# Opening the bilinear layer in the experts' memory slots: the change, the profile before it, and what it should do to the time

## The chip, the core and the metric

The kernel is one program on one core of a Trainium2 chip. The core has a matrix engine (TensorE, here PE), a vector engine (VectorE, DVE), an activation engine (ScalarE, ACT), a general engine (GpSimd, POOL) and a queue engine that issues transfers (SyncE, SP); each runs its own instructions in order, and they wait for each other through semaphores. Operands lie in on-chip memory in tiles, which are taken from pools: a pool has a fixed number of slots for a tag, and a new tile of that tag waits until the last reader of the tile that had the slot is done. The metric is device time in microseconds (us) of one launch, median of several runs.

## The reference

Three layers follow each other: attention of 8 batches against 32 state rows, a mixture of 8 experts in which each of 4352 rows goes to one expert, and the bilinear layer, with which this document is mostly concerned.

```
def _moe_ref(x, w_gate, w_output_gate, w1, w2):      # x: 4352 x 512
    ...                                               # e_idx: the expert of each row, with two gates
        h = np.maximum(x[mask] @ w1[e], 0.0)          # 512 -> 1024
        ye = h @ w2[e]                                # 1024 -> 512
        out[mask] = gate_w[mask, None] * eom[mask, e, None] * ye
def _moe2_ref(x, w1, w2, w3, w_out):
    a = x @ w1                                        # 512 -> 1024
    b = x @ w2
    h = a * b @ w3                                    # 1024 -> 1024
    return (h @ w_out).astype(np.float32)             # 1024 -> 512
```

Everything is float32, but for the weights of the bilinear layer, which are passed as float64.

## The kernel before, in words

**Arithmetic.** A float32 product is made of three PE passes over halves: `split` (L177, L178) makes a rounded half on ACT (a CAST) and the remainder on DVE, and `passes` (L183) multiplies high by high, high by low and low by high. The two last matrices of the bilinear layer are multiplied together beforehand (`wo`, 1024 x 512), beside the attention.

**Experts.** Rows are sorted by expert and worked through in 10 units. A unit has a first matrix (`ph`, L183 into relu at L1013 and L1014) and a second (`py`). The results are copied by ACT to a tile `y` (L1064 in the last unit, L1076 in the others) and written to the array `y_T` by transfers that ACT issues. Expert weights are loaded raw by SP into `wr_raw` (tag `raw`, 3 slots) and split into pairs of half tiles of 128x2x512 elements, which lie in two rings of slots, `wr0` (8 pairs) and `wr1` (4 pairs). Rows are gathered into tiles `xg` (4 slots).

**Bilinear operands.** `operands()` works in the gaps of the experts: in 16 steps it loads a piece of w1 and w2 as raw 64-bit words, converts it (L218 and L232 on ACT, more on DVE and POOL; tiles `wab`), forms the sums that the seven-product scheme of Strassen and Winograd wants, splits them (`wh_w`, `wh_s`) and writes them to `w_rows`, one row for each of the 8 values of f.

**Bilinear layer.** The 34 tiles of 128 rows are worked through in 5 blocks of 7, 7, 7, 7 and 6. `load_y` (L1254) loads a block of `y_T` in two tiles; `sums_of` (L1362) forms four differences t1 to t4 (on DVE in block 0, on POOL later) and splits seven operands x0 to x6. For each f (8 per block), `load_w` (L1332) brings the 1.79 MB of `w_rows` for that f (2 slots, each taken by the load two steps ahead), and `products` makes 7 products p1 to p7 of 6 PE passes each (42 matmuls of 448 columns), combines them (u2, u3, u4, a1, b1 on DVE; b2 L1412, a2 L1415 and the product `ab` L1416 on POOL; s1 and s5 are copied by ACT, L1403 and L1406) and splits `ab` in two parts: `aa` for 4 of the row tiles and `ab` for the others. `out_of` multiplies these by `wo` (`po`, 512 columns): 4 tiles x 3 passes = 12 per f follow one step of f behind, the other row tiles come at the end of the block. `written` scales a row tile to `o` (L1439 on ACT, L1441 on DVE; in a slot of `xg`) and scatters it to the output with a transfer that POOL issues (L1442).

**Memory and order.** The pools of the experts (`c3`, `c4`) are closed before the bilinear layer, whose nine pools `bl0` to `bl8` lie where they were. So a bilinear tile waits for those readers of expert tiles whose memory it has. The order of instructions on each engine is set when the program is built, by a scheduler that estimates when each is ready.

Of the kernel before, what the change touches and what calls it, by code (L numbers as in the profile page):

```python
# [9 lines left out]
F32 = mybir.dt.float32  # L10
# [42 lines left out]
def tile_attention_moe_bilinear(  # L53
# [137 lines left out]
    def load_f32(pool, name, src, tag, bufs, temps=None, tmp=2):  # L191

        src = src if isinstance(src, list) else [src]
# [12 lines left out]
        if not wide:  # L206
            return w
        words = raw.bitcast(I32).rearrange("p (n t) -> p n t", t=2)
# [94 lines left out]
    with ExitStack() as c1:  # L303
# [388 lines left out]
        c3 = ctx.enter_context(ExitStack())  # L692
        rings.append(Lines(c3.enter_context(tc.tile_pool(name="wr0", bufs=RING0, reuse_waits="tile"))))
# [176 lines left out]
    rings.append(Lines(c3.enter_context(tc.tile_pool(name="wr1", bufs=RING - RING0, reuse_waits="tile"))))  # L870
# [14 lines left out]
    with ExitStack() as c2:  # L885
# [56 lines left out]
        def operands():  # L942

            for f in range(KF):
                for kk in range(2):
                    wa_, wb_ = [
                        w.rearrange("(h m p) f -> m p h f", h=2, p=P)[kk][:, :, f * P : (f + 1) * P]
                        for w in (wa, wb)
                    ]
                    name = f"{f}_{kk}"  # L950
                    w = load_f32(
                        e3, "wab" + name, [wa_, wb_[:, 1], wb_[:, 0]], "wab", 1, None, 1
                    ).rearrange("p (m n) -> p m n", n=P)
                    a11, a12, a22, a21 = [w[:, i] for i in range(4)]
                    yield
                    sums = e3.tile([P, 4, P], F32, tag="top", name="sums" + name, bufs=1)
                    s1, s2, s3, s4 = [sums[:, i] for i in range(4)]
                    add = nc.gpsimd.tensor_tensor
                    add(s1, a21, a22, op=ALU.add)
                    add(s3, a11, a21, op=ALU.subtract)  # L960
                    add(s2, s1, a11, op=ALU.subtract)
                    add(s4, a12, s2, op=ALU.subtract)
                    halves(w[:, 0:3], (f, kk, 0), "w" + name)
                    yield
                    write_wab()
                    yield
                    halves(sums, (f, kk, 3), "s" + name)
                    yield
                    write_wab()
# [276 lines left out]

        def load_y(s):
# [64 lines left out]
    c3.close()  # L1312


    def bilinear(y, group):
# [5 lines left out]
        with ExitStack() as c5:  # L1321
            wp, ap, xp0, op0, xp1, op1, aap, abp, tp = [
                Lines(c5.enter_context(tc.tile_pool(name=f"bl{i}{group}", bufs=1, reuse_waits="tile")))
                for i in range(9)
            ]
            NB = max(BLOCKS) * P
            NH = NB // 2
            w_t, wo, raw_wo = {}, {}, {}

            def load_w(s, f):  # L1330
                t = wp.tile([P, 2, 2, NP, P], F32R, tag="w", name=f"w{s}_{f}", bufs=2)
                nc.sync.dma_start(out=t.bitcast(F32), in_=w_rows[f])  # L1332
                w_t[s, f] = t

            def load_wo(f):
                raw_wo[f] = wr_raw.tile([P, DM], F32, tag="raw", name=f"rwo{f}", bufs=RAW)
                nc.sync.dma_start(out=raw_wo[f], in_=wo_rows[f * P : (f + 1) * P])

            def split_wo(f):
                wo[f] = [  # L1340
                    p.tile([P, DM], F32R, tag="wo", name=f"wo{j}_{f}", bufs=KF)
                    for j, p in enumerate((op0, op1))
                ]
                split(*wo[f], raw_wo.pop(f))

            def sums_of(y, s):

                n = BLOCKS[s] * P // 2
                b11, b21, b12, b22 = [h[:, i : i + 2] for h in y for i in (0, 2)]
                x = {}  # L1350

                def put(i, src):
                    hl = [
                        (xp0 if i < 2 else xp1).tile([P, 2, NH], F32R, tag=f"x{i}_{j}", name=f"x{i}_{j}_{s}")
                        for j in range(2)
                    ]
                    x[i] = both(hl, slice(None), slice(None), slice(0, n))
                    split(*x[i], src)

                def less(i, a, b):  # L1360
                    t = wr_raw.tile([P, 2, NH], F32, tag="raw", name=f"t{i}_{s}", bufs=RAW)[:, :, 0:n]
                    (nc.vector if s == 0 else nc.gpsimd).tensor_tensor(t, a, b, op=ALU.subtract)  # L1362
                    return t

                t1 = less(1, b12, b11)
                t2 = less(2, b22, t1)
                put(0, b11)
                put(1, t1)
                t3 = less(3, b22, b12)
                put(2, t2)  # L1370
                t4 = less(4, t2, b21)
                put(3, t3)
                put(4, b21)
                put(5, b22)
                put(6, t4)
                return x

            A11, A12, A22, S1, S2, S3, S4 = range(NP)
# [165 lines left out]
```

## Time and profile before

| | us |
|---|---|
| runs | 1183.18, 1186.32, 1191.93 (median 1186.32) |
| profiled execution | 1187.32 |
| its span | 1185.4 |
| PE busy in the span | 1123.0 |
| granted clock of PE over the span | 0.982 of full speed |

The span is the time from the first to the last instruction that the profiler saw; the profiled execution took 1.9 us more than that. In the profile's views every instruction has the line of the source and the tiles it writes and reads (`p<-x,w`), a count of instructions (`x42`) and, in brackets, the idle time of the engine before it with what ended that. Rows of one kind that follow each other are put together. The experts lie from before 215 us to 634 us, the bilinear layer from 634 us to the end.

### The profile page before, as it was taken

How to read it: one execution, taken by the hardware profiler on the slowest of the kernel's cores; microseconds unless marked ns; L12 is line 12 of the kernel's file. 1: busy time of each engine (PE TensorE's matmuls, PEld its weight loads, DVE VectorE, ACT ScalarE, POOL GpSimd, SP SyncE). 2: the span in 40 equal slices, each digit the busy share in tenths (PEclk: the TensorE clock that was granted, in tenths of full speed). 3: DMA queues.
4: the chain of work that ended last, by engine and by line, in shares of the span. 5: the costliest groups of instructions: out<-in, count | busy, mean ns of one | idle time of the engine just before them, and what ended most of it. 6: DMA issues, size and time to landing. Idle time of an engine off the chain costs nothing. (4 is left out here: it accounts for less than half of the span.)

```text
span 1185.4 us, 18194 instructions
## 1 busy us (share of the span) xinstructions
PE 1123.0 (95%) x6880; PEld 986.2 (83%) x6880; DVE 660.9 (56%) x1206; ACT 448.7 (38%) x807; POOL 396.3 (33%) x383
## 2 busy tenths in 40 slices
PE   5888999999989999999997999999999999999994
PEld 4665777999989999878885888888888889889993
DVE  4999797535554647464752746343634544463441
ACT  3788544435454545454213223211321222132110
POOL 2655335113220412141000534532463363334331
PEclk9999999999999999999997999999999999999997
DMA  7776427547575666676114654544544445444431
GB/s 223 235 246 215 142 90 242 179 152 233 180 239 192 218 201 222 225 243 202 54 63 178 240 186 141 207 161 175 186 186 145 168 177 187 137 174 143 175 118 56
DMA packets 83040, 211.55 MB, mean 178 GB/s; under 512 B 12928, under 2 KB 40576, under 8 KB 77824
## 3 DMA queue, kind: packets, MB, share of 16 engines
q1 hardware_dynamic: 60288, 167.53, 41.2%
q10 hardware_dynamic: 17024, 24.42, 5.6%
q0 software_dynamic: 5632, 18.35, 4.6%
q8 instruction: 56, 0.92, 0.3%
q14 instruction: 40, 0.33, 0.1%
HBM read 166.23 MB, written 44.04 MB: 177 GB/s over the span
## 5 line engine op out<-in xcount | busy, mean ns | idle before, releaser
L183 PE MATMUL p<-x,w 128*128 128x448 f32 (+1 forms) x1680 | 350.2, 363 | 8.7 <-DMA w<-w_rows 7.1
L183 PEld LDWEIGHTS p<-x,w 128*128 128x128 f32 x1680 | 315.2, 190 | 35.9 <-issue 7.5
L183 PE MATMUL py<-h,w 128*128 128x288 f32 (+1 forms) x1152 | 199.6, 331 | 6.1 <-ACT y L1076 6.0
L183 PE MATMUL ph<-x,w 128*128 128x288 f32 (+2 forms) x1248 | 195.3, 316 | 0.8 <-DVE h L1014 0.8
L183 PEld LDWEIGHTS py<-h,w 128*128 128x128 f32 x1152 | 175.5, 190 | 22.5 <-ACT y L1076 7.7
L183 PEld LDWEIGHTS ph<-x,w 128*128 128x128 f32 x1248 | 179.4, 188 | 12.5 <-DVE h L1014 1.2
L1412 POOL TENSOR_TENSOR b<-u,s 128x448 f32<-128x448 f32 (+1 forms) x40 | 47.7, 1191 | 279.5 <-DVE u L1411 279.5
L178 DVE TENSOR_TENSOR w<-raw,w 128x1024 fp32r<-128x1024 f32 x80 | 96.7, 1236 | 76.0 <-ACT w L177 75.4
L183 PE MATMUL po<-wo,aa 128*128 128x512 f32 x480 | 123.1, 393 | 0.9 <-ACT aa L177 0.9
L183 PEld LDWEIGHTS po<-wo,aa 128*128 128x128 f32 x480 | 89.7, 188 | 18.0 <-ACT aa L177 1.5
L177 ACT CAST w<-raw 128x1024 fp32r<-128x1024 f32 x80 | 81.6, 1050 | 50.6 <-DMA raw<-in_moe_w 45.7
L177 ACT CAST ab<-ab 128x384 fp32r<-128x384 f32 (+1 forms) x40 | 19.7, 492 | 210.1 <-POOL ab L1416 210.1
L233 POOL TENSOR_TENSOR wab<-wab,wab_top 128x512 int32<-128x512 int32 x16 | 20.6, 1287 | 187.2 <-DVE wab_top L226 177.5
L183 PE MATMUL po<-wo,ab 128*128 128x512 f32 x336 | 79.6, 390 | 0.0
L183 PEld LDWEIGHTS po<-wo,ab 128*128 128x128 f32 x336 | 62.9, 188 | 13.3 <-DVE o L1441 0.2
L986 POOL DMA_INDIRECT xg<-x_rows,gidx x38 | 44.0, 1158 | 81.0 <-PE pxg L992 75.3
L1415 POOL TENSOR_TENSOR a<-u,s 128x448 f32<-128x448 f32 (+1 forms) x40 | 48.4, 1209 | 58.8 <-DVE u L1414 58.7
L1014 DVE SCALAR_TENSOR_TENSOR h<-ph,h 128x288 fp32r<-128x288 f32 (+2 forms) x104 | 51.1, 501 | 20.2 <-ACT h L1013 19.6
L1414 DVE TENSOR_TENSOR u<-u,p 128x448 f32<-128x448 f32 (+1 forms) x40 | 24.3, 607 | 64.1 <-PE p L183 63.9
L1013 ACT ACTIVATE h<-ph 128x288 fp32r<-128x288 f32 (+2 forms) x104 | 44.4, 446 | 40.3 <-PE ph L183 28.1
L183 PE MATMUL pwo<-wu,w3T 128*128 128x512 f32 x192 | 50.5, 413 | 3.4 <-POOL w3T L178 2.9
L1416 POOL TENSOR_TENSOR ab<-a,b 128x448 f32<-128x448 f32 (+1 forms) x40 | 50.1, 1252 | 3.1
(289 smaller groups left out, 1411.9 us busy)
## 6 DMA issues: line engine op xcount, KB each, us to landing
w<-w_rows SPq DMA_DIRECT2D x40, 1792.0 KB, 7.1
raw<-in_moe_w SPq DMA_DIRECT2D x80, 512.0 KB, 4.3
x<-in_x SPq DMA_DIRECT2D x32, 256.0 KB, 5.6
w_raw<-in_moe_w SPq DMA_DIRECT2D x16, 512.0 KB, 4.1
x_rows<-xr SPq DMA_DIRECT2D x32, 256.0 KB, 2.8
w_rows<-wh_s ACTq DMA_DIRECT2D x32, 256.0 KB, 2.0
y<-y_T SPq DMA_DIRECT2D x8, 896.0 KB, 6.6
w_rows<-wh_w ACTq DMA_DIRECT2D x32, 192.0 KB, 3.3
```

The source lines that it names most:

```text
L177: nc.scalar.copy(hi, src)
L178: (engine or nc.vector).tensor_tensor(lo, src, hi.bitcast(F32), op=ALU.subtract)
L183: m = nc.tensor.matmul(o, l[a], r[b], start=start and i == 0, stop=stop and i == 2)
L233: nc.gpsimd.tensor_tensor(wi, wi, top, op=ALU.add)
L986: gathered = nc.gpsimd.indirect_dma_start(out=x[0:r], out_offset=None, in_=x_rows, in_offset=bass.IndirectOffsetOnAxis(ap=gidx[0:r, t - s0 ...
L1013: nc.scalar.activation(hl[0], src, AF.Relu)
L1014: nc.vector.scalar_tensor_tensor(out=hl[1], in0=src, scalar=0.0, in1=hl[0].bitcast(F32), op0=ALU.max, op1=ALU.subtract)
L1412: gpsimd(b2, u3, s5, op=ALU.add)
L1414: vector(u4, u2, p3, op=ALU.add)
L1415: gpsimd(a2, u4, s5, op=ALU.add)
L1416: gpsimd(ab[:, n : 2 * n], a2, b2, op=ALU.mult)
```

## The change

The rings `wr0` and `wr1` stay open to the end, and five of the nine bilinear pools are gone. The operands x0 to x6 and the differences take pairs of slots in ring `wr0` (9 allocations per block on 8 slots), `wo` takes ring `wr1`, the raw `wo` rows and the temporaries u3 and u4 take `xg` slots (shared with output rows `o`), and a1, b1, a2, b2 and `ab` take `wr_raw` slots. A new `begin()` runs ahead of the last expert unit's second matrix: it loads block 0 of y, the `w_rows` of f = 0 in four pieces (three into `wr_raw`, one into `xg`) and makes the first half of block 0's operands. The bilinear layer then starts with the loads of f = 1 and f = 2. In `operands()` the raw load stands one gap ahead of its conversion. The code for more rows than usual takes the same calls and is left out below.

```diff
@@ load_f32 is split; the raw load can now stand apart from the conversion @@
+        return convert(*load_raw(pool, name, src, tag, bufs), pool, name, temps)
+
+    def load_raw(pool, name, src, tag, bufs):
...
+        return w, raw
+
+    def convert(w, raw, pool, name, temps=None):
+        if raw is w:
             return w
+        n = w.shape[1]
...
-        c3 = ctx.enter_context(ExitStack())
-        rings.append(Lines(c3.enter_context(tc.tile_pool(name="wr0", bufs=RING0, reuse_waits="tile"))))
+        rings.append(Lines(ctx.enter_context(tc.tile_pool(name="wr0", bufs=RING0, reuse_waits="tile"))))
...
-    rings.append(Lines(c3.enter_context(tc.tile_pool(name="wr1", bufs=RING - RING0, reuse_waits="tile"))))
+    rings.append(Lines(ctx.enter_context(tc.tile_pool(name="wr1", bufs=RING - RING0, reuse_waits="tile"))))
...
@@ operands @@
+            def loaded(f, kk):
...
+                return load_raw(e3, f"wab{f}_{kk}", [wa_, wb_[:, 1], wb_[:, 0]], "wab", 1)
+
+            each = list(itertools.product(range(KF), range(2)))
+            raw = loaded(*each[0])
+            yield
+            for i, (f, kk) in enumerate(each):
+                name = f"{f}_{kk}"
+                w = convert(*raw, e3, "wab" + name).rearrange("p (m n) -> p m n", n=P)
+                a11, a12, a22, a21 = [w[:, i] for i in range(4)]
+                yield
...
+                halves(w[:, 0:3], (f, kk, 0), "w" + name)
+                yield
+                write_wab()
+                if i + 1 < len(each):
+                    raw = loaded(*each[i + 1])
+                yield
+                halves(sums, (f, kk, 3), "s" + name)
+                yield
+                write_wab()
...
+        def pair(i, name):
+            return [rings[i].tile([P, 2, 512], F32R, tag=f"w{j}", name=f"w{j}_{name}") for j in range(2)]
+
...
+        def sums_of(y, s, x):
+
+            n = BLOCKS[s] * P // 2
+            b11, b21, b12, b22 = [h[:, i : i + 2] for h in y for i in (0, 2)]
+            less = lambda o, a, b: (nc.vector if s == 0 else nc.gpsimd).tensor_tensor(o, a, b, op=ALU.subtract)
+
+            def put(i, src):
+                x[i] = both(pair(0, f"x{i}_{s}"), slice(None), slice(None), slice(0, n))
+                split(*x[i], src)
+
+            t1, t2 = [t[:, :, 0:n].bitcast(F32) for t in pair(0, f"t12_{s}")]
+            less(t1, b12, b11)
+            less(t2, b22, t1)
+            put(0, b11)
+            put(1, t1)
+            put(2, t2)
+            yield
+            t3, t4 = [t[:, :, 0:n].bitcast(F32) for t in pair(0, f"t34_{s}")]
+            less(t3, b22, b12)
+            less(t4, t2, b21)
+            put(3, t3)
+            put(5, b22)
+            put(4, b21)
+            put(6, t4)
+
+        def begin():
+
+            y = load_y(0)
+            w = {}
+            for first, n in ((S1, 2), (S3, 2), (A11, 2), (A22, 1)):
+                if n == 2:
+                    t = wr_raw.tile([P, 2, 2, 2, P], F32R, tag="raw", name=f"wf{first}", bufs=RAW)
+                else:
+                    t = xp.tile([P, 2, 2, 1, P], F32R, tag="xg", name=f"wf{first}", bufs=BX)
+                nc.sync.dma_start(out=t.bitcast(F32), in_=w_rows[0][:, :, :, first : first + n])
+                w.update({first + i: t[:, :, :, i] for i in range(n)})
+            x = {}
+            todo = sums_of(y, 0, x)
+            next(todo)
+            return w, x, todo
...
-                    y0 = load_y(0)
                     for _ in fills:
                         pass
+                    begun = begin()
                 second_of(n)
...
-    c3.close()
...
-            wp, ap, xp0, op0, xp1, op1, aap, abp, tp = [
+            wp, tp, aap, abp = [
...
             def load_wo(f):
-                raw_wo[f] = wr_raw.tile([P, DM], F32, tag="raw", name=f"rwo{f}", bufs=RAW)
+                raw_wo[f] = xp.tile([P, DM], F32, tag="xg", name=f"rwo{f}", bufs=BX)
...
             def split_wo(f):
...
+                if f % 2 == 0:
+                    hl = pair(1, f"wo{f}")
+                    wo.update({f + i: both(hl, slice(None), i) for i in range(2)})
                 split(*wo[f], raw_wo.pop(f))
...
+                def temp(pool, tag, name, bufs=1):
+                    return pool.tile([P, 512], F32, tag=tag, name=f"{name}_{s}_{f}", bufs=bufs)[:, 0:n]
+
+                def temps(name):
+                    t = wr_raw.tile([P, 2, 512], F32, tag="raw", name=f"{name}_{s}_{f}", bufs=RAW)
+                    return t[:, 0, 0:n], t[:, 1, 0:n]
...
+                u3 = temp(xp, "xg", "u3", BX)
                 vector(u3, u2, p7, op=ALU.add)
+                a2, b2 = temps("ab2")
...
+                u4 = temp(xp, "xg", "u4", BX)
...
+                ab = wr_raw.tile([P, 1024], F32, tag="raw", name=f"ab_{s}_{f}", bufs=RAW)
...
+                a1, b1 = temps("ab1")
...
-            load_w(0, 0)
-            x = sums_of(y, 0)
             load_w(0, 1)
-            for f in range(RAW):
+            load_w(0, 2)
+            for _ in todo:
+                pass
+            for f in range(2):
                 load_wo(f)
...
-                        if f + RAW < KF:
-                            load_wo(f + RAW)
+                        if f + 2 < KF:
+                            load_wo(f + 2)
...
-                    if f + 2 < KF or more:
+                    if (f + 2 < KF or more) and (s or f):
...
-                    x = sums_of(y, s + 1)
+                    x = {}
+                    for _ in sums_of(y, s + 1, x):
+                        pass
...
-    bilinear(y0, "out")
+    bilinear(*begun, "out")
```

In the order of instructions, SP's rows at the end of the experts' loads, before (`raw_7` is the last expert's last weight, `y` and `w` belong to block 0, `rwo` is a raw row block of `wo`):

```order
301 L875 DMA raw_7_7044<-in_moe_w 128x2x512
302 L1254 DMA y_1_7425<-y_T 128x4x448
303 L1254 DMA y_0_7423<-y_T 128x4x448
304 L1332 DMA w_0_7579<-w_rows 128x3584
305 L1332 DMA w_1_7617<-w_rows 128x3584
306 L1337 DMA rwo_7619<-wo_rows 128x512
307 L1337 DMA rwo_7621<-wo_rows 128x512
```

and with the change (`wf` are the four pieces for f = 0):

```order
301 L881 DMA raw_7_7036<-in_moe_w 128x2x512
302 L1310 DMA wf_7433<-w_rows 128x4x128
303 L1310 DMA wf_7427<-w_rows 128x4x256
304 L1310 DMA wf_7429<-w_rows 128x4x256
305 L1310 DMA wf_7431<-w_rows 128x4x256
306 L1394 DMA rwo_7610<-wo_rows 128x512
307 L1394 DMA rwo_7612<-wo_rows 128x512
308 L1273 DMA y_1_7425<-y_T 128x4x448
309 L1273 DMA y_0_7423<-y_T 128x4x448
310 L1389 DMA w_1_7586<-w_rows 128x3584
311 L1389 DMA w_2_7588<-w_rows 128x3584
```

The four pieces and two `rwo` loads now stand ahead of the y loads, and the first whole `w` loads are those of f = 1 and 2.

ACT's rows in one expert unit (338 to 361 us of the trace), before (`wab_1` is an operand step, `py_0_288` the second column half of the unit's first output group, `raw` and `w` are weights of the coming unit):

```order
413 L1076 COPY y_0_4514<-py_0_0_4515 128x288
414 L177 CAST w_2_3_4501<-raw_3_4499 128x1024
415 L177 CAST x_12_4425<-pxg_4447 128x4x128
416 L177 CAST x_12_4425<-pxg_4456 128x4x128
417 L218 ACTIVATE wab_1_top<-wab_1_raw 128x512
418 L232 ACTIVATE wab_1_4683<-wab_1_raw 128x512
419 L1076 COPY y_0_4514<-py_0_288_4541 128x288
420 L1078 REGISTER_ALU
421 L1078 DMA y_T<-y_0_4514 128x576
422 L1076 COPY y_1_4570<-py_1_0_4571 128x288
```

and with the change:

```order
410 L177 CAST wh_s_0_4682<-sums_0_4558 128x512
411 L1087 COPY y_0_4505<-py_0_0_4506 128x288
412 L945 DMA w_rows<-wh_s_0_4682 128x512
413 L177 CAST x_12_4416<-pxg_4438 128x4x128
414 L177 CAST w_2_3_4492<-raw_3_4490 128x1024
415 L177 CAST x_12_4416<-pxg_4447 128x4x128
416 L945 DMA w_rows<-wh_s_0_4683 128x512
417 L1087 COPY y_0_4505<-py_0_288_4532 128x288
418 L225 ACTIVATE wab_1_top<-wab_1_raw 128x512
419 L239 ACTIVATE wab_1_4623<-wab_1_raw 128x512
```

The second copy of `y_0` stood behind both `wab_1` instructions and now stands ahead of them; a cast `wh_s_0` of the operand step before now stands ahead of the first copy.

POOL's rows at the end of block 0, before (`b`, `a` and `ab` with `_0_7` or `_7` belong to f = 7, `t_1` to block 1, `t_2` to block 2):

```order
227 L1412 TENSOR_TENSOR b_0_7_8308<-u_0_7_8303,s_0_7_8326 128x448
228 L1362 TENSOR_TENSOR t_1_8417<-t_1_8401,y_0_7813 128x896
229 L1415 TENSOR_TENSOR a_0_7_8306<-u_0_7_8304,s_0_7_8326 128x448
230 L1416 TENSOR_TENSOR ab_7_8309<-a_0_7_8306,b_0_7_8308 128x448
231 L1362 TENSOR_TENSOR t_2_9275<-y_1_8721,y_0_8719 128x896
232 L1442 DMA out<-o_8482,L 4352x512
233 L1442 DMA out<-o_8488,L 4352x512
234 L1442 DMA out<-o_8494,L 4352x512
235 L1362 TENSOR_TENSOR t_2_9277<-y_1_8721,t_2_9275 128x896
236 L1362 TENSOR_TENSOR t_2_9287<-y_1_8721 128x896
237 L1442 DMA out<-o_8500,L 4352x512
238 L1442 DMA out<-o_8506,L 4352x512
```

and with the change (`ab_0_7` stands for b2 and then a2; `w_t_1` are t3 and t4 of block 1 in a ring pair):

```order
226 L1280 TENSOR_TENSOR w_t_1_8380<-y_1_7796 128x2x448
227 L1280 TENSOR_TENSOR w_t_1_8381<-w_t_1_8365,y_0_7794 128x2x448
228 L1434 TENSOR_TENSOR ab_0_7_8308<-u_0_7_8306,s_0_7_8288 128x448
229 L1438 TENSOR_TENSOR ab_0_7_8308<-u_0_7_8317,s_0_7_8288 128x448
230 L1440 TENSOR_TENSOR ab_7_8320<-ab_0_7_8308 128x448
231 L1280 TENSOR_TENSOR w_t_2_9224<-y_1_8682,y_0_8680 128x2x448
232 L1467 DMA out<-o_8447,L 4352x512
233 L1467 DMA out<-o_8453,L 4352x512
234 L1280 TENSOR_TENSOR w_t_2_9225<-y_1_8682,w_t_2_9224 128x2x448
235 L1467 DMA out<-o_8459,L 4352x512
236 L1467 DMA out<-o_8465,L 4352x512
237 L1467 DMA out<-o_8471,L 4352x512
```

Before, one difference stood behind b2 of f = 7; now two stand ahead of it, and among the scatters there are two differences of block 2 (t1, t2) where there were three.

## Rows read from the trace of the kernel before

**Rows 1.** The page, part 1: busy time (us), share of span, instructions.

```profile
PE 1123.0 (95%) x6880; PEld 986.2 (83%) x6880; DVE 660.9 (56%) x1206; ACT 448.7 (38%) x807; POOL 396.3 (33%) x383
```

**Rows 2.** Waits of PE over the whole span: total us, times, longest us.

```profile
PE p L183 <- DMA w<-w_rows: 7.1, 1, 7.1
PE py L183 <- ACT y L1076: 6.0, 7, 2.5
```

**Rows 3.** Windows: busy us per engine, granted clock, DMA share, GB/s.

```profile
640.00:660.00 20.00, 17.41 (x59) 14.92 (x60) 9.85 (x13) 6.50 (x9) 3.82 (x3) 0.66 0.81 291
```

**Rows 4.** PE timeline: start, us, instruction, count, idle before; experts into bilinear layer.

```profile
621.19 12.74 PE L183 MATMUL py<-h,w 128*128 128x512 f32 x55
641.03 4.82 PE L183 MATMUL p<-x,w 128*128 128x448 f32 x12 [7.11 <-DMA w<-w_rows]
647.31 14.40 PE L183 MATMUL p<-x,w 128*128 128x448 f32 x54 [1.46 <-ACT x L177]
662.58 2.33 PE L183 MATMUL po<-wo,aa 128*128 128x512 f32 x9 [0.88 <-ACT aa L177]
...
685.37 2.44 PE L183 MATMUL po<-wo,aa 128*128 128x512 f32 x10
```

**Rows 5.** PE timeline: two later f steps of block 0.

```profile
696.71 2.48 PE L183 MATMUL po<-wo,aa 128*128 128x512 f32 x10
...
703.14 5.11 PE L183 MATMUL p<-x,w 128*128 128x448 f32 x24
708.08 2.48 PE L183 MATMUL po<-wo,aa 128*128 128x512 f32 x10
```

**Rows 6.** SP timeline: issues of the first weight loads.

```profile
633.79 0.83 SPq L1332 DMA_DIRECT2D w<-w_rows  x2
```

**Rows 7.** ACT timeline in the same stretch: issue of the first y_T write.

```profile
632.55 0.34 ACTq L1065 DMA_DIRECT2D y_T<-y  x1
```

**Rows 8.** DMA issues, 625 to 660 us: count, KB each, median us to landing.

```profile
y_T<-y ACTq DMA_DIRECT2D x4, 256.0 KB, 2.3
```

**Rows 9.** PE timeline inside one expert unit, 338 to 361 us.

```profile
343.10 3.42 PE L183 MATMUL py<-h,w 128*128 128x288 f32 x24 [0.51 <-ACT y L1076]
...
349.54 11.34 PE L183 MATMUL py<-h,w 128*128 128x288 f32 x72 [2.49 <-ACT y L1076]
```

**Rows 10.** ACT timeline beside it.

```profile
347.98 0.66 ACT L218 ACTIVATE wab_top<-wab_raw 128x512 f32<-128x512 f32 x1 [2.42 <-DMA wab_raw<-in_moe_w]
...
349.09 0.39 ACT L1076 COPY y<-py 128x288 f32<-128x288 f32 x1
```

**Rows 11.** POOL timeline at the end of block 0.

```profile
731.82 1.84 POOL L1412 TENSOR_TENSOR b<-u,s 128x448 f32<-128x448 f32 x1 [5.55 <-DVE u L1411]
733.62 2.97 POOL L1362 TENSOR_TENSOR t<-t,y 128x896 f32<-128x896 f32 x1
736.56 2.01 POOL L1415 TENSOR_TENSOR a<-u,s 128x448 f32<-128x448 f32 x1
738.65 1.89 POOL L1416 TENSOR_TENSOR ab<-a,b 128x448 f32<-128x448 f32 x1
749.57 2.12 POOL L1362 TENSOR_TENSOR t<-y,y 128x896 f32<-128x896 f32 x1 [9.03 <-DMA y<-y_T]
```

**Rows 12.** DVE timeline there.

```profile
730.01 1.09 DVE L178 TENSOR_TENSOR x<-y,x 128x896 fp32r<-128x896 f32 x1
731.03 0.62 DVE L1411 TENSOR_TENSOR u<-u,p 128x448 f32<-128x448 f32 x1
...
735.76 1.78 DVE L178 TENSOR_TENSOR x<-y,x 128x896 fp32r<-128x896 f32 x1 [0.36 <-ACT x L177]
...
754.76 0.75 DVE L1441 TENSOR_SCALAR o<-po,L 128x512 f32<-128x512 f32 x1 [3.69 <-DMA out<-o,L]
```

**Rows 13.** ACT timeline there.

```profile
740.57 0.52 ACT L177 CAST ab<-ab 128x384 fp32r<-128x384 f32 x1 [2.35 <-POOL ab L1416]
```

**Rows 14.** PE timeline there.

```profile
737.25 4.94 PE L183 MATMUL po<-wo,ab 128*128 128x512 f32 x21
```

More of the change, by code (lines that the diff above doesn't have):

```diff
@@ L205, in load_f32 @@
             nc.sync.dma_start(out=o, in_=a)
-        if not wide:
+        return w, raw
+    def convert(w, raw, pool, name, temps=None):
+        if raw is w:
             return w
+        n = w.shape[1]
         words = raw.bitcast(I32).rearrange("p (n t) -> p n t", t=2)
@@ L942, in operands @@
         def operands():
[L944 to L969, printed above, removed]
@@ new lines, in loaded @@
+            def loaded(f, kk):
+                wa_, wb_ = [
+                    w.rearrange("(h m p) f -> m p h f", h=2, p=P)[kk][:, :, f * P : (f + 1) * P]
+                    for w in (wa, wb)
+                ]
+                return load_raw(e3, f"wab{f}_{kk}", [wa_, wb_[:, 1], wb_[:, 0]], "wab", 1)
[7 more added lines that the diff above has]
+                yield
+                sums = e3.tile([P, 4, P], F32, tag="top", name="sums" + name, bufs=1)
+                s1, s2, s3, s4 = [sums[:, i] for i in range(4)]
+                add = nc.gpsimd.tensor_tensor
+                add(s1, a21, a22, op=ALU.add)
+                add(s3, a11, a21, op=ALU.subtract)
+                add(s2, s1, a11, op=ALU.subtract)
+                add(s4, a12, s2, op=ALU.subtract)
+                halves(w[:, 0:3], (f, kk, 0), "w" + name)
[7 more added lines that the diff above has]
+                write_wab()
@@ L1245, in tile_attention_moe_bilinear @@
         fills = itertools.chain(operands(), places())
+        NB = max(BLOCKS) * P
+        NH = NB // 2
+        A11, A12, A22, S1, S2, S3, S4 = range(NP)
+        def pair(i, name):
+            return [rings[i].tile([P, 2, 512], F32R, tag=f"w{j}", name=f"w{j}_{name}") for j in range(2)]
         def load_y(s):
@@ L1311, in tile_attention_moe_bilinear, with bilinear @@
         c4.close()
-    c3.close()
-    def bilinear(y, group):
+    def bilinear(w0, x, todo, group):
         with ExitStack() as c5:
-            wp, ap, xp0, op0, xp1, op1, aap, abp, tp = [
+            wp, tp, aap, abp = [
                 Lines(c5.enter_context(tc.tile_pool(name=f"bl{i}{group}", bufs=1, reuse_waits="tile")))
-                for i in range(9)
+                for i in range(4)
             ]
-            NB = max(BLOCKS) * P
-            NH = NB // 2
-            w_t, wo, raw_wo = {}, {}, {}
+            w_t, wo, raw_wo = {(0, 0): w0}, {}, {}
             def load_w(s, f):
@@ L1332, in load_w @@
                 nc.sync.dma_start(out=t.bitcast(F32), in_=w_rows[f])
-                w_t[s, f] = t
+                w_t[s, f] = [t[:, :, :, c] for c in range(NP)]
             def load_wo(f):
-                raw_wo[f] = wr_raw.tile([P, DM], F32, tag="raw", name=f"rwo{f}", bufs=RAW)
+                raw_wo[f] = xp.tile([P, DM], F32, tag="xg", name=f"rwo{f}", bufs=BX)
                 nc.sync.dma_start(out=raw_wo[f], in_=wo_rows[f * P : (f + 1) * P])
             def split_wo(f):
[L1340 to L1343, printed above, removed]
+                if f % 2 == 0:
+                    hl = pair(1, f"wo{f}")
+                    wo.update({f + i: both(hl, slice(None), i) for i in range(2)})
                 split(*wo[f], raw_wo.pop(f))
[L1346 to L1378, printed above, removed]
             def products(s, f, x):
@@ L1383, in products @@
                 w = w_t.pop((s, f))
-                def temp(pool, name, tag=None):
-                    return pool.tile([P, 512], F32, tag=tag or name, name=f"{name}_{s}_{f}", bufs=1)[:, 0:n]
                 def product(i, tag, c, name):
@@ L1512, in tile_attention_moe_bilinear @@
                 run(range(T0 + FEW, MAXT))
-        bilinear(load_y(0), "again")
+        bilinear(*begin(), "again")
 _INS = [
```

12 lines of the change are left out of this document (3 added, 9 removed).

## The prediction

> **What bounds the kernel now.** I read the busy times first: PE is busy 1123.0 of 1185.4 us [rows 1], so at most 62.4 us of waiting can go, and whatever is gained elsewhere only counts where PE waits for it. The list of PE's waits comes next. Most of its entries belong to the attention, which the change leaves alone; the two that it touches are the longest of all, 7.1 us for the first `w` of the bilinear layer, and 6.0 us in 7 pieces for ACT's copies of expert results, the longest 2.5 us [rows 2]. The windows add what waits alone don't tell: around 634 us PE is not only idle, its granted clock is 0.66 on the mean of 640 to 660 us, between the levels of 1.2 and 2.4 GHz [rows 3]. From 663.5 us to the end of the layer PE has no idle time, so there the change can only cost.
>
> The sum is made against the profiled execution, 1187.3 us, which is 1.0 above the median of the runs shown (1186.3).
>
> **1. From the experts into the bilinear layer.** The last `py` ends at 621.19 + 12.74 = 633.93. SP issues the two first `w` loads at 633.79, since their slots lie on expert memory that `py` still reads [rows 6], and the first product starts at 641.03, 7.24 us after that issue [rows 4]. Then PE waits 7.11, 1.46 and 0.88 us and runs slowly in between: 12 matmuls in 4.82 us [rows 4].
>
> How much of this stretch is work? By 685.37, where the `po` of f = 2 begin, PE has done f = 0, 1, 2 and the first 24 products of f = 3, and the `po` of f = 0 and 1: 150 products and 24 `po`. A later step (42 products, 12 `po`) takes 708.08 - 696.71 = 11.37 us; 24 products start at 703.14 and the next `po` at 708.08, so 4.94 us for 24 or 0.206 each, and the 12 `po` are 11.37 - 42 x 0.206 = 2.72 [rows 5]. Three steps, 24 products more and one set of `po` less: 3 x 11.37 + 4.94 - 2.72 = 36.3 us. It took 685.37 - 633.93 = 51.4. **15.1 us** can be won at most: 9.45 idle, the other 5.7 the low clock.
>
> With the change, the four pieces for f = 0 are issued ahead of the y loads, all the splits of block 0's operands stand on ACT ahead of the last `y` copies, and PE goes from the last `py` matmul into p1. Is the next thing late? f = 1 needs a whole `w` at 633.93 + 42 x 0.206 = 642.6. Its load still waits for `py`, is issued at about 633.9 and can be had 7.2 us later, at 641.1: 1.5 us to spare. f = 2 needs its load 11.4 us after that, and in the trace the second of two loads issued together held nothing up. The copies s1 and s5 now stand on ACT among the four `y` copies, of which there are two buffers: the third waits for the first transfer, issued at 632.55 [rows 7] and landed 2.3 us later [rows 8], 634.9; s1 follows at about 636 and PE wants it at 633.93 + 24 x 0.206 = 638.9. Two `rwo` blocks and the rest of `wo` are off the path. I take 14.5 us of the 15.1, 0.6 for a late piece; bounds 0 and 15.1. A loss is excluded, because the old loads at the old time are the worst that can be left.
>
> **2. The experts.** PE waits 2.49 us at 347.05 for a copy of `y` [rows 9]; ACT stood before `wab_top`, which waited 2.42 us for its raw words, and made the copy only at 349.09 [rows 10]. With the change that copy stands ahead of both `wab` instructions, so this wait goes. The 72 matmuls behind it took 11.34 us where 24 take 3.42 [rows 9], so 11.34 - 10.26 = 1.1 us of low clock may go too. On the other side the cast `wh_s` of the step before now stands ahead of the first copy. A cast of 384 columns takes 0.52 us [rows 13], so one of 512 some 0.6 by estimate, and the wait of 0.51 at 343.10 may grow by that. The raw transfers stay in their order on SP. Between 0 and -3.6 I take **-2.5 us**, about the value of the named wait plus half of what the clock and the new cast leave.
>
> **3. The ends of the blocks (4 times).** t3 and t4 of the next block now stand ahead of b2 of f = 7 on POOL, where only t4 stood behind it. In the trace u3 was made at 731.03 [rows 12] and POOL went b2 1.84, t4 2.97, a2 2.01, `ab` 1.89 [rows 11], and ACT cast at 740.57 [rows 13]. t3's slot comes free with p7, just ahead of u3, at about 730.9. A difference takes 2.12 alone and 2.97 beside DVE [rows 11]. So the chain ends after 2 x 2.12 to 2 x 2.97, then 1.84 to 2.01, 2.01 and 1.89: at 740.9 to 742.8, and the cast of 0.52 at 741.4 to 743.3. In the order with the change PE has 21 `po` and 8 products before it wants that cast; the 21 begin at 737.25 and end at 742.1 [rows 14], so with 8 x 0.206 at 743.75. The slack is 0.4 to 2.3 us. I cost this at 0; without that cover it is up to 2.97 each time.
>
> Next, u3 and u4 take `xg` slots that rows `o` also take, and wait for scatters. DVE has already waited 3.69 us there for one, with PE busy [rows 12]. Behind it on DVE stands u2 and everything PE's product banks wait for. Since t1 and t2 only, not three differences, now stand between the scatters, the fourth is issued at least 2.12 us earlier than before, which covers it. I put 0.2 us on each end, **+0.8** in all, out of 0 to 4 x (2.97 + 3.69) = 26.6.
>
> By the Trainium skill (SBUF — State Buffer, "SBUF: two separate sides") VectorE instructions with two on-chip inputs and GpSimd ones hold a shared pair of ports as an exclusive lock, and the other blocks fully. The trace agrees that they disturb each other, 1.09 against 1.78 us for a DVE remainder [rows 12]; by a full block the chain here would be longer than I sum it, and that is the third rival.
>
> **Sum.** 1187.3 - 14.5 - 2.5 + 0.8 = 1171.1, say **1171 us**; own range 1167 to 1175.
>
> **Rivals.**
> - *Half of the first gain stays away.* The clock is low anyway, or f = 1 waits because its load shares the transfer engines with the `y_T` writes. For: slack of only 1.5 us; DMA share 0.81 in the window that follows [rows 3]. Against: those writes ran beside the first `w` before as well. 1171.1 + 7.2 = 1178.
> - *Operands for f = 0 are not early.* The change doesn't do what it says if a piece waits for a slot until the last `py`. Then 7.1 us and the low clock stay, and only the expert part is won: 1187.3 - 2.5 = 1185. Against: the order has the pieces ahead of the y loads, and those ahead of the first whole `w`.
> - *Full blocking between DVE and POOL at the ends.* Four late remainders (x3, x5, x4, x6) of 1.09 us alternate with the five POOL instructions, so the chain is 4.4 us longer; less 0.8 of slack, 3.6 four times: 1171.1 + 14.4 = 1185. For: 1.78 instead of 1.09, 2.97 instead of 2.12. Against: these durations, in a stretch just like it, are already in my sum.
> - *Slower: scatters hold the next block's u3.* Place: DVE's first u3 of blocks 1 to 4. If the `ab` of f = 7 comes 2.97 late and u3 then finds its slot under a scatter still on its way, 3.69 more, PE stops behind full banks and pays the low clock, 1.1 as after the 2.49 us wait: 7.8 us four times is 31: 1202. It decides once the slack of 0.4 us is used up and a scatter lands more than about 2 us later than before.
>
> **Chances.** Forecast 0.63, half gain 0.14, not early 0.06, blocking 0.08, scatters 0.09. A measurement of this kernel can tell about 1%, 11.9 us. Faster by more needs less than 1174.4: nearly all of the forecast and a little of the half gain, 0.64. Within 1%: 0.28. Slower by over 1%: 0.08, the scatters. The range takes in the forecast with both of its ends, the half gain and part of the two at 1185: low 1171.1 - 0.6 - 1.1 - 0.8 - 3 for the spread of the runs, about 1165; high 1184.
>
> **What would show it.** Right: no wait of PE for `w` or `x` near 634, a granted clock near 1.00 from 620 to 660, PE at the `po` of f = 2 some 36.3 us after the last `py`; no 2.5 us wait in the expert unit; no PE idle at the four block ends. Wrong: a wait `p <- w` at about 642, `p <- s` at 639, `po <- ab` at a block end, or DVE waiting for `out` ahead of a u3 with PE idle behind it.

## The result and the profile after

The changed kernel takes **1171.74 us** (median of 4 runs, 1168.13 to 1172.81) where the kernel before takes 1186.97 beside it (4 runs): ratio 0.9864, 95% interval 0.9821 to 0.9907. The forecast was 1171. The profiled execution took 1172.32, its span 1170.1, so 15.3 us are gone from the span.

On the page, PE's busy time fell by 3.9 us [rows 1]; the rest of the 15.3 is waiting that is gone.

```profile
PE 1119.1 (96%) x6880; PEld 983.0 (84%) x6880; DVE 664.0 (57%) x1206; ACT 449.7 (38%) x807; POOL 397.0 (34%) x383
```

The list of PE's waits has no entry for `w` or `x` any more, and `py` is down from 6.0 us to 2.2 [rows 2]. `ph` has grown from 0.8 us to 2.8, and `po` has two waits, 1.0 and 0.8, where it had one of 0.9 [rows 4].

```profile
PE ph L183 <- DVE h L1025: 2.8, 4, 0.9
...
PE py L183 <- ACT y L1087: 2.2, 4, 1.0
...
PE po L183 <- ACT aa L177: 1.0, 1, 1.0
PE po L183 <- DVE aa L178: 0.8, 1, 0.8
```

**From the experts into the bilinear layer.** The windows of this stretch show the clock at its upper level throughout (the last three values are the clock, the DMA share and GB/s), where 640 to 660 us had 0.66 [rows 3].

```profile
620.00:640.00 20.00, 20.00 (x95) 17.43 (x94) 10.71 (x17) 7.00 (x10) 2.98 (x3) 1.00 0.46 173
640.00:660.00 20.00, 18.18 (x84) 15.39 (x84) 12.71 (x16) 5.76 (x11) 8.50 (x6) 1.00 0.76 288
```

PE's timeline answers to [rows 4]: from the last `py` PE goes straight into the 42 products of f = 0 (`wf` are the four early pieces) and the next 24, and the `po` of f = 2 begin at 669.71, which is 38.59 us after the last `py` (631.12) instead of 51.44. Here and below, where the products follow the last `py` at once, its end is taken as their start; the end that the profile models for it is 0.16 us later, so a start with a wait and one without can be compared only to within that.

```profile
619.90 11.38 PE L183 MATMUL py<-h,w 128*128 128x512 f32 x49
631.12 8.68 PE L183 MATMUL p<-w_x,wf 128*128 128x448 f32 x42
639.63 5.02 PE L183 MATMUL p<-w_x,w 128*128 128x448 f32 x24
645.64 1.22 PE L183 MATMUL po<-w_wo,aa 128*128 128x512 f32 x3 [0.98 <-ACT aa L177]
...
659.24 0.73 PE L183 MATMUL po<-w_wo,aa 128*128 128x512 f32 x2 [0.84 <-DVE aa L178]
...
669.71 2.23 PE L183 MATMUL po<-w_wo,aa 128*128 128x512 f32 x9
```

Who was late for the two `po`? For the first, ACT's timeline tells: the cast of `ab` and the cast `aa` behind it stood 10.27 us for a write of `y_T`, although the last such write had been issued at 633.89.

```profile
633.89 0.34 ACTq L1076 DMA_DIRECT2D y_T<-y  x1
644.55 0.51 ACT L177 CAST ab<-ab 128x384 fp32r<-128x384 f32 x1 [10.27 <-DMA y_T<-y]
644.97 0.61 ACT L177 CAST aa<-ab 128x512 fp32r<-128x512 f32 x1
```

SP had issued two whole `w` at 631.35 [rows 6], 2.5 us ahead of that write; the first y_T write was issued at 629.90, as early against the last `py` as in [rows 7]. The list of transfers of 625 to 662 us has the four writes at a median of 6.3 us, against 2.3 before [rows 8]. Neither median stands for all four: asked write by write, the trace with the change gives a landing for two, 2.1 us for the first, issued ahead of the loads, and 10.6 for the last; the trace before gives one, 2.3 for the write issued at 633.60, ahead of the loads, and none for the two issued behind them.

```profile
631.35 0.82 SPq L1389 DMA_DIRECT2D w<-w_rows  x2
```
```profile
y_T<-y ACTq DMA_DIRECT2D x4, 256.0 KB, 6.3
```

The second `po` has another cause. ACT's cast `aa` for it ends at 655.1; DVE is late with the remainder, because two remainders ahead of it took 2.49 and 2.61 us beside POOL's first two differences of block 1. With POOL idle such remainders take 0.56 us (at 711.02) and 0.69 (at 651.23). The remainder of `aa` then ends at 659.18, and PE goes on at 659.24.

```profile
653.36 2.27 POOL L1280 TENSOR_TENSOR w_t<-y,y 128x896 f32<-128x896 f32 x1 [2.14 <-DMA y<-y_T]
653.56 2.49 DVE L178 TENSOR_TENSOR ab<-ab,ab 128x384 fp32r<-128x384 f32 x1
655.71 2.32 POOL L1280 TENSOR_TENSOR w_t<-y,w_t 128x896 f32<-128x896 f32 x1
655.98 2.61 DVE L178 TENSOR_TENSOR w_wo<-rwo,w_wo 128x512 fp32r<-128x512 f32 x1
```

**The experts.** The `py` of [rows 9] runs without its wait, and its 72 matmuls take 10.13 us instead of 11.34. The price is in the next unit, where PE waits for `h`, and ACT stands twice ahead of a relu (`h`): for the raw words, 2.58 us where it was 1.24 before (at 382.64, with no wait of PE), and in the cast `wh_s` for a write of `w_rows`, 2.07 us.

```profile
345.81 6.88 PE L183 MATMUL py<-h,w 128*128 128x288 f32 x50
...
352.66 10.13 PE L183 MATMUL py<-h,w 128*128 128x288 f32 x72
...
381.72 8.22 PE L183 MATMUL ph<-x,w 128*128 128x288 f32 x60 [0.92 <-DVE h L1025]
390.87 4.38 PE L183 MATMUL ph<-x,w 128*128 128x288 f32 x31 [0.93 <-DVE h L1025]
```
```profile
380.17 0.67 ACT L225 ACTIVATE wab_top<-wab_raw 128x512 f32<-128x512 f32 x1 [2.58 <-DMA wab_raw<-in_moe_w]
380.73 0.40 ACT L1024 ACTIVATE h<-ph 128x288 fp32r<-128x288 f32 x1
...
388.83 0.62 ACT L177 CAST wh_s<-sums 128x512 fp32r<-128x512 f32 x1 [2.07 <-DMA w_rows<-wh_w]
```

**The end of block 0.** POOL now does t3, t4, b2, a2 and `ab` in a row, which answers to [rows 11]; ACT casts `ab` at 726.23 to 726.74, and PE wants it at 727.82 and has no idle time: 1.1 us to spare [rows 13, 14].

```profile
715.25 2.12 POOL L1280 TENSOR_TENSOR w_t<-y 128x896 f32<-128x896 f32 x1 [4.80 <-PE p L183]
717.33 2.97 POOL L1280 TENSOR_TENSOR w_t<-w_t,y 128x896 f32<-128x896 f32 x1
720.26 2.01 POOL L1434 TENSOR_TENSOR ab<-u,s 128x448 f32<-128x448 f32 x1
722.23 2.00 POOL L1438 TENSOR_TENSOR ab<-u,s 128x448 f32<-128x448 f32 x1
724.30 1.89 POOL L1440 TENSOR_TENSOR ab<-ab 128x448 f32<-128x448 f32 x1
```
```profile
726.23 0.51 ACT L177 CAST ab<-ab 128x384 fp32r<-128x384 f32 x1 [3.17 <-POOL ab L1440]
```
```profile
721.42 4.95 PE L183 MATMUL po<-w_wo,ab 128*128 128x512 f32 x21
726.20 1.78 PE L183 MATMUL p<-w_x,w 128*128 128x448 f32 x8
727.82 5.17 PE L183 MATMUL po<-w_wo,ab 128*128 128x512 f32 x22
```

DVE beside it (answers to [rows 12]); the scatter still costs DVE some 3 us, at an `o`, not at a u3:

```profile
715.74 2.58 DVE L178 TENSOR_TENSOR w_x<-w_t,w_x 128x896 fp32r<-128x896 f32 x1
719.05 2.20 DVE L178 TENSOR_TENSOR w_x<-w_t,w_x 128x896 fp32r<-128x896 f32 x1 [0.73 <-PE p L183]
...
738.92 0.75 DVE L1466 TENSOR_SCALAR o<-po,L 128x512 f32<-128x512 f32 x1 [3.10 <-DMA out<-o,L]
```

### The profile page after: what moved, and what is told of

It reads as the page before. It is cut to its first block, busy times and chain, and to the rows that moved or that the text cites. A ratio compares the mean times of both kernels' runs of the same rounds, so it can differ in the third digit from the quotient of the medians.

```text
span 1170.1 us, 18224 instructions
## 1 busy us (share of the span) xinstructions
PE 1119.1 (96%) x6880; PEld 983.0 (84%) x6880; DVE 664.0 (57%) x1206; ACT 449.7 (38%) x807; POOL 397.0 (34%) x383
## 5 line engine op out<-in xcount | busy, mean ns | idle before, releaser
L183 PE MATMUL p<-w_x,w 128*128 128x448 f32 (+1 forms) x1638 | 338.5, 359 | 0.0
L183 PEld LDWEIGHTS p<-w_x,w 128*128 128x128 f32 x1638 | 303.7, 188 | 25.3
L1434 POOL TENSOR_TENSOR ab<-u,s 128x448 f32<-128x448 f32 (+1 forms) x40 | 47.5, 1188 | 259.8 <-DVE u L1432 170.8
L183 PE MATMUL po<-w_wo,aa 128*128 128x512 f32 x480 | 125.3, 393 | 1.8 <-ACT aa L177 1.0
L183 PEld LDWEIGHTS po<-w_wo,aa 128*128 128x128 f32 x480 | 89.7, 188 | 18.8 <-DVE aa L178 1.7
L183 PE MATMUL po<-w_wo,ab 128*128 128x512 f32 x336 | 79.6, 391 | 0.0
L183 PEld LDWEIGHTS po<-w_wo,ab 128*128 128x128 f32 x336 | 62.9, 188 | 13.4 <-ACT o L1464 0.3
L1438 POOL TENSOR_TENSOR ab<-u,s 128x448 f32<-128x448 f32 (+1 forms) x40 | 48.3, 1208 | 49.2 <-DVE u L1437 49.2
L1440 POOL TENSOR_TENSOR ab<-ab 128x448 f32<-128x448 f32 (+1 forms) x40 | 48.9, 1221 | 3.1
```

Source lines behind the costliest of these rows:

```text
L183: m = nc.tensor.matmul(o, l[a], r[b], start=start and i == 0, stop=stop and i == 2)
L1434: gpsimd(b2, u3, s5, op=ALU.add)
L1438: gpsimd(a2, u4, s5, op=ALU.add)
L1440: gpsimd(ab[:, n : 2 * n], a2, b2, op=ALU.mult)
```

## The experiments

PE's timeline gives three lengths that can be compared between profiles, all in us: *experts* from the first `py` of 512 columns to the end of the last one, *start* from there to the `po` of f = 2, and *rest* from there to the end of PE's last instruction. Below they decide more than the medians, whose intervals are some 5 to 10 us wide.

| kernel | experts | start | rest | median, ratio to before [95%] |
|---|---|---|---|---|
| before | 409.64 | 51.44 | 483.33 | |
| the change | 407.15 | 38.59 | 483.60 | 1171.74, 0.9864 [0.9821, 0.9907] |
| the change, again | 406.18 | 38.70 | 483.43 | 1170.63, 0.9877 [0.9857, 0.9898] |
| late `w` | 405.17 | 47.42 | 483.41 | 1179.03, 0.9961 [0.9940, 0.9983] |
| late operands | 404.67 | 40.24 | 483.40 | 1170.29, 0.9894 [0.9851, 0.9938] |
| old fills | 409.25 | 38.49 | 483.39 | 1172.22, 0.9901 [0.9867, 0.9935] |
| new fills alone | 407.68 | 50.98 | 483.16 | 1181.08, 0.9977 [0.9957, 0.9996] |

### The first weights at their old time

The pools stay as in the change; the four early pieces are gone and f = 0 has a whole `w` again.

```diff
-            for first, n in ((S1, 2), (S3, 2), (A11, 2), (A22, 1)):
...
-            w_t, wo, raw_wo = {(0, 0): w0}, {}, {}
+            w_t, wo, raw_wo = {}, {}, {}
...
+            load_w(0, 0)
             load_w(0, 1)
-            load_w(0, 2)
...
-                    if (f + 2 < KF or more) and (s or f):
+                    if f + 2 < KF or more:
```

> The changed kernel, but the weights of f = 0 come as one whole load at the bilinear layer's start, as before; the operands x stay early. Theory (the gain at the start is the wait for w and the low clock behind it): PE idles about 7 us after the last py, the granted clock falls again, and from the last py to the po of f = 2 it takes 47 to 49 us instead of 38.6; 1180 to 1182 us in all. Rival (x, not w, held the start): within 2 us of 1172.

1179.03 us, a little under what was expected, and the wait is back on PE:

```profile
636.41 15.45 PE L183 MATMUL p<-w_x,w 128*128 128x448 f32 x66 [7.53 <-DMA w<-w_rows]
```

Behind it the 66 products take 0.234 us each instead of 0.207, and the window says 0.83:

```profile
620.00:640.00 20.00, 12.47 (x50) 10.25 (x49) 5.52 (x9) 5.33 (x8) 0.00 (x0) 0.83 0.58 222
```

The start takes 47.42 us. So of the 12.85 that the change wins there, 47.42 - 38.59 = 8.8 hang on the four early pieces, the other 4.0 on what was early besides.

### The operands x later

All of block 0's operands are now ordered behind the last unit's second copy of `y`; none is begun ahead.

```diff
+                    copied.append(nc.scalar.copy(y[:, 0:n], po[f]))
...
             todo = sums_of(y, 0, x)
-            next(todo)
             return w, x, todo
...
-            for _ in todo:
-                pass
+            with tc.issue_after(copied[1].ins) if group == "out" else ExitStack():
+                for _ in todo:
+                    pass
```

> The changed kernel, but ACT's casts of block 0's operands x are queued behind the second of the last unit's y copies, about where they stood before; the four weight pieces stay early. Theory (x is the smaller half of the start): the first product waits about 2 us for x0, then the casts at 0.95 us each keep ahead of products at 1.23 us each, and the copies behind them are late once: 3 to 5 us more than the change, 1175 to 1177. Rival (x early is worth nothing, because ACT would be in time anyway): within 1 us of 1172. Other rival (x is as much as w): 1179 or more.

The start is 40.24 us, only 1.65 longer than with the change; the three new waits of PE are short, because ACT's casts of 0.87 to 0.98 us keep just ahead of the products:

```profile
627.32 0.47 PE L183 MATMUL p<-w_x,wf 128*128 128x448 f32 x1 [0.53 <-ACT w_x L177]
628.15 4.06 PE L183 MATMUL p<-w_x,wf 128*128 128x448 f32 x18 [0.37 <-ACT w_x L177]
632.45 5.05 PE L183 MATMUL p<-w_x,wf 128*128 128x448 f32 x23 [0.24 <-DVE w_x L178]
```

That is less than was expected: early operands are worth little by themselves. The early weights carry the start. The two experiments give 8.8 and 1.65 of the 12.85 us; some 2.4 are lost in neither, so they need only one of the two to be early, or hang on the open slots themselves, which no run keeps without an early load.

### The fills: the old ones in the change, the new ones alone

The first kernel is the change with the old loop of `operands()`, which loads and converts in one step; the second is the kernel before with the new loop and nothing else.

```diff
-            raw = loaded(*each[0])
-            yield
-            for i, (f, kk) in enumerate(each):
-                w = convert(*raw, e3, "wab" + name).rearrange("p (m n) -> p m n", n=P)
...
+            for f in range(KF):
+                for kk in range(2):
...
+                    w = load_f32(
+                        e3, "wab" + name, [wa_, wb_[:, 1], wb_[:, 0]], "wab", 1, None, 1
+                    ).rearrange("p (m n) -> p m n", n=P)
```

> The changed kernel with the operand steps as before (raw load and conversion in one gap). Theory (the experts' part of the gain is this edit alone): the 2.5 us wait for ACT's y copy is back, the three new waits of 0.2, 0.9 and 0.9 us for relu are gone, the last py ends some 2.5 us later, 1174 us in all; from the last py on nothing changes (38.6 us to the po of f = 2). Rival (the slots that stay open moved the experts): the last py ends where it does with the change.

> The kernel before with the new operand steps and nothing else. Theory: the last py ends 2.5 us earlier than before and the rest is as before (51.4 us to the po of f = 2): 1184 to 1185. Rival (it needs the open slots): as before, 1187.

Each does one half. With the old fills the wait of the expert unit is back and the 72 matmuls behind it take 11.33 us again, while the start stays at 38.49. The time of 1172.22 is below the 1174 expected and cannot be told from the change's:

```profile
347.50 11.33 PE L183 MATMUL py<-h,w 128*128 128x288 f32 x72 [1.88 <-ACT y L1082]
```

With the new fills alone the start stays long, 50.98 us with its wait of 7.11, and the kernel gains 3.0 us in the median (0.9977, 0.9957 to 0.9996). Experts with old fills: 409.64 and 409.25; with the new: 407.15, 406.18 and 407.68, 405.17 and 404.67 in the two kernels above, and 408.30, 405.12, 406.00, 406.01 and 404.00 in the five below, whose edits all lie behind the experts. Against the one profile before, the new fills are thus worth 1.3 to 5.6 us. How much stays goes with PE's waits for `h` and `y`: together they are 3.0 us where the experts take 404.00, 5.0 in the change and 6.5 where they take 408.30. The longest, 1.97 us when the change was run again and 2.08 in *both* below, come where `wh_s` stood 4.0 us for its write of `w_rows`.

### POOL's t4 made twice

Five blocks have four ends; at each, POOL gets one difference more, to use up the slack.

```diff
             less(t4, t2, b21)
+            if s:
+                less(t4, t2, b21)
```

> The changed kernel with t4 of each coming block computed twice on POOL (same value), the second time ahead of a2 of f = 7. Theory (the chain b2, a2, ab of f = 7 has 1.1 us of slack at a block end, as the changed kernel's trace shows at the first one): it grows by 2.1 to 3.0 us, PE waits 1.0 to 1.9 us for the cast of ab at each of the four ends, 4 to 8 us in all, seen as waits of po for ACT ab. Rival (the ends have much more cover than that, since the scheduler finds other products to put first): no wait of PE, same time.

1176.81 us, ratio 0.992 (0.9892 to 0.9947); the rest grows to 488.39, by 4.8. The size is as expected, the place is not. PE waits four times, not for ACT's cast of `ab` but for DVE's a1 (L1445), which frees a bank of products:

```profile
729.99 1.49 PE L183 MATMUL p<-w_x,w 128*128 128x448 f32 x6 [1.11 <-DVE ab L1445]
```

DVE was late because its remainders ran beside POOL, and because one of them, 1.89 us, now stands ahead of a1; in the change a1 (725.10) stands ahead of that remainder (726.16):

```profile
723.01 4.44 DVE L178 TENSOR_TENSOR w_x<-y,w_x 128x896 fp32r<-128x896 f32 x2
727.52 1.89 DVE L178 TENSOR_TENSOR w_x<-w_t,w_x 128x896 fp32r<-128x896 f32 x1
729.33 0.61 DVE L1445 TENSOR_TENSOR ab<-s,p 128x448 f32<-128x448 f32 x1
```

ACT's cast of `ab` ends at 730.96, and PE, with 12 products ahead of those `po` instead of 8, takes it at 731.32 without a wait. So the ends are covered in the change, and one difference of 2.97 us, together with the order that the scheduler made for it, uses the cover up: it cost 1.2 per end.

### Where the last 2 us of the start are

The floor is 36.3 us and the start takes 38.59. Three edits ask what makes `aa` late. In *pools*, `abp` and `aap` trade places, so that the first casts do not lie on the last copies' memory. In *w behind y*, the `w` of f = 2 is loaded behind block 1 of y and no longer directly behind the `w` of f = 1. *Both* has the two edits.

```diff
-            wp, tp, aap, abp = [
+            wp, tp, abp, aap = [
```
```diff
             load_w(0, 1)
-            load_w(0, 2)
...
+                    if f == (1 if s else 0) and more:
                         y = load_y(s + 1)
+                    if f + 2 < KF or more:
+                        with tc.issue_after(loads[-1].ins) if s + f == 0 else ExitStack():
+                            load_w(*((s, f + 2) if f + 2 < KF else (s + 1, f + 2 - KF)))
```

> The changed kernel with the pools abp and aap in the other order, so that the halves of the first f lie no longer on the last unit's y tiles. Theory (the 2.3 us that the start still loses against 36.3 come from ACT's first ab cast waiting for the y_T writes): the cast comes at about 9.5 instead of 13.4 us after the last py, the 0.98 us wait of po goes, and from the last py to the po of f = 2 it takes 37.0 to 37.6 instead of 38.6 us. Rival (the late rwo blocks set it): the 0.84 us wait and a total of 38.6 stay, the loss only moves.

> The changed kernel with the whole load of f = 2 queued on SP behind block 1's y loads, so that only one whole load shares the transfer engines with the last y_T writes. Theory (the writes land late because two loads of 1.8 MB are ahead of them): they land within about 5 us instead of 10, ACT's first ab cast is no longer held, the rwo blocks come earlier, and the stretch takes 36.5 to 37.5 us. Rival (f = 2 then comes late): a wait of p for w of 1 to 4 us at about 21 us after the last py.

> Both of these edits. Theory: the stretch from the last py to the po of f = 2 takes 36.3 to 37.0 us, 1.6 to 2.3 less than the change; in time about 1.5 to 2 us less, which the runs can hardly tell. Rival: as with the load of f = 2 moved alone, if it comes late.

None comes into the range expected for it. In each the first wait goes and another comes: `ab` is cast 9.4 us after the last `py` with *pools* and 9.6 us with *w behind y*, instead of 13.4. *Pools* (1172.75, 0.9889, 0.9858 to 0.992; start 40.36): ACT stands before the split of a raw `wo` row that has not landed, with the next `aa` behind it, and DVE's remainder of `aa` then takes 2.56 us beside a difference on POOL. PE's wait grows to 2.23 us, and the 18 products behind it take 5.09 us instead of 3.81, at a granted clock of 0.55 from 658.7 to 661 us.

```profile
654.11 0.62 ACT L177 CAST w_wo<-rwo 128x512 fp32r<-128x512 f32 x1 [3.08 <-DMA rwo<-wo_rows]
656.11 2.56 DVE L178 TENSOR_TENSOR aa<-ab,aa 128x512 fp32r<-128x512 f32 x1
```
```profile
658.73 1.09 PE L183 MATMUL po<-w_wo,aa 128*128 128x512 f32 x2 [2.23 <-DVE aa L178]
```

*W behind y* (1169.81, 0.9871, 0.9842 to 0.99; start 38.27): the last write is issued at 631.50 and lands 6.7 us later instead of 10.6. So the second `w` had held the writes up, but now that `w` itself is late for PE. *Both* (1169.03, 0.9857, 0.9832 to 0.9883; start 39.64) has the same wait, and a stretch of low clock behind it, 0.60 from 652 to 656 us: 7.88 us for the 30 products that take 6.32 in the other.

```profile
650.78 6.32 PE L183 MATMUL p<-w_x,w 128*128 128x448 f32 x30 [1.91 <-DMA w<-w_rows]
```
```profile
652.33 7.88 PE L183 MATMUL p<-w_x,w 128*128 128x448 f32 x30 [1.81 <-DMA w<-w_rows]
```

### An order that puts the second weights in between

SP's order becomes `w` of f = 1, two rows of `wo`, `w` of f = 2, and then block 1 of y. The change itself ran beside it on the same chip.

```diff
             load_w(0, 1)
-            load_w(0, 2)
...
+                        if f == 0:
+                            with tc.issue_after(issued["wo"].ins):
+                                load_w(0, 2)
+                            second = issued["w"]
...
-                        y = load_y(s + 1)
+                        with tc.issue_after(second.ins) if s == 0 else ExitStack():
+                            y = load_y(s + 1)
```

> The changed kernel with another order of SP's loads at the start: the whole load of f = 1, the rwo blocks of f = 2 and 3, then the whole load of f = 2, then block 1's y loads. Theory (the start loses 2.3 us because the y_T writes stand behind two whole loads, and the run with the load of f = 2 behind the y loads lost 1.9 us because it came too late): the load of f = 2 is issued when p4 of f = 0 has ended, 8.7 us after the last py, and lands 7 us later, 6 us ahead of its use; the writes land as early as in that run; the stretch from the last py to the po of f = 2 takes 36.3 to 37.0 us and PE has no wait in it. In time 1.5 to 2.3 us less than the change. Rival (something else is late next, an rwo block or block 1's y): a new wait of PE of 1 us or more there or at the end of block 0.

> The changed kernel as it is, beside the kernel above on one chip. The last py ends 405 to 409 us after the first, the stretch behind it takes 38.6 us again, with the two waits of 1.0 and 0.8 us, and the ratio to the kernel before is 0.985 to 0.988.

Start 37.26 us, the shortest of all and 0.26 above the range expected, with one wait of 0.79 left; the second `w` is issued at 638.70, behind two `wo` rows that waited for a slot, and still comes in time; the last write lands 8.1 us after its issue at 632.40. Behind the wait that is left stands again DVE's remainder of `aa`, 2.61 us beside a difference on POOL.

```profile
630.23 8.41 SPq L1395 DMA_DIRECT2D rwo<-wo_rows  x2
638.70 0.56 SPq L1390 DMA_DIRECT2D w<-w_rows  x1
```
```profile
656.48 0.50 PE L183 MATMUL po<-w_wo,aa 128*128 128x512 f32 x1 [0.79 <-DVE aa L178]
```

1168.52 us (5 runs, 0.9873, 0.9844 to 0.9903) against 1170.63 for the change (6 runs, 0.9877, 0.9857 to 0.9898). The 1.4 us show in the start; in the time the two cannot be told apart.

## Why the prediction was right

The total came out as forecast, 1171.74 for 1171; of 16.2 us by the sum, 15.3 showed in the span: 12.85 in the start and 2.49 in the experts, less 0.27 in the rest; 0.3 lies ahead of the experts, where the change does nothing. By its steps:

- **The start: 14.5 forecast, 12.85 measured.** The mechanism is as predicted: no wait for `w` or `x`, the clock at its upper level. Of the 15.1 us that could be won, the late `w` experiment gives 8.8 to the early pieces alone. What was mis-sized is the late piece, 0.6 us in the sum and 2.3 in the profile, of which 1.82 is waiting. It was looked for at `w` of f = 1 and at the copies s1 and s5, and none of these was late. The first wait, 0.98, comes from the writes of `y_T`. I priced them at the 2.3 us of [rows 8], which is the landing of one write issued ahead of the loads, and asked only which copies wait for them. But the first `ab` lies on the memory of the last copies, the writes went out behind two loads of 1.8 MB, and the last landed 10.6 us after its issue. *Pools* and *w behind y*, each of which brings the cast forward by some 4 us against the last `py`, show one half of that each. The second wait, 0.84, comes from DVE's remainders beside POOL's differences. That is read from the rows; no run moves these differences alone. The blocking of the third rival was sought only at the block ends.
- **The experts: 2.5 forecast, 2.49 measured, and that was partly luck.** The named wait went with its low clock, as predicted: 2.49 + 1.21. The term itself was loose: 2.49 and half of what 1.1 and 0.6 leave would be 2.7. What I left out is the next unit: there ACT's waits for the raw words and for a write of `w_rows` stand ahead of relu, and cost PE 2 us in the change in pieces of 0.2 to 0.9. Over ten profiles the gain is 1.3 to 5.6 us. What decides when the raw words and that write land was not tried and stays open.
- **The ends: 0.8 forecast, 0.1 to 0.3 measured.** The slack of the cast at the first end is 1.1 us, inside the predicted 0.4 to 2.3. The doubled difference shows that the ends have less than 3 us of cover; what ran out there was not this slack but a1 on DVE, which the prediction did not price.
- **The rivals.** Half the gain and operands that are not early are refuted by the start. Scatters that hold u3: DVE waited 3.10 us, but at an `o`, with PE busy. The price of full blocking did not come at the ends. The mechanism did: t3 ends at 717.37 and the DVE remainder that began at 715.74 ends 0.95 later, at 718.32; t4 ends 1.98 after that, at 720.30; the next remainder ends 0.95 after that. Each does nearly its whole work after the other's end: alone a remainder takes 1.09 us and a difference 2.12. By the Trainium skill (SBUF — State Buffer, "SBUF: two separate sides") the two share a pair of ports as an exclusive lock; these rows agree. The rival erred in adding it to durations, 2.97 and 1.78, which already held it.

## What to carry to other kernels

Where one phase of a kernel waits for the memory of the one before, look first for the operand that the new phase starts with: the first weights alone, loaded early into slots that were free, won 8.8 of 12.85 us here, and more than the wait itself of 7.5, since the clock was low behind it. Then ask of every tile that takes old memory what the last user of that memory is: if it is a transfer, price its landing behind the loads that now run beside it, not as it was measured ahead of them. And a wait taken away from one instruction of an engine that works in order can come back ahead of a later one: look who stands behind it there.

## What was not expected of the hardware

- A write of 256 KB on ACT's queue landed 10.6 us after its issue when two loads of 1792 KB had been issued on SP's queue 2.5 us earlier, and 6.6 to 8.1 us with one such load ahead. In the same trace as the 10.6, a write issued ahead of the loads landed after 2.1.
- Remainders on DVE of 0.56 and 0.69 us took 2.49 and 2.61 beside differences on POOL, and PE waited 0.84 us for what stood behind them.
- The clock after waits of similar length differs: behind 1.91 us of waiting 30 products took 6.32 us at a granted clock of 1.00, behind 1.81 they took 7.88, with 0.60 at their start. In the experts, 48 `ph` matmuls took 8.15 us behind 1.97 and 6.63 behind 2.08. What makes the difference stays open. After waits of up to 1.0 us in the change it stayed at 1.00; after 7.53 it was 0.83 on the mean of the window, and 66 products took 15.45 us instead of 13.7.
